# 29 unread products on TensorE behind the last y product, some on strips of 32 partitions

## The chip, the core and the metric

The kernel runs on one core of a Trainium2 chip. Its engines work side by side and are tied by semaphores: TensorE (PE) multiplies matrices, VectorE (DVE), ScalarE (ACT) and GpSimd (POOL) work on elements, and SyncE (SP) issues most of the DMAs. The metric is the device time of one execution in microseconds (us).

## The reference

The input `x` has 2048 tokens of 512 features. It is normalised (`xn`), and two branches work on that:

```
xn = layernorm(x)
h[t] = Lam_bar * h[t-1] + xn[t] @ B_bar.T          # 512 complex states, over all 2048 tokens
s  = 2 * real(h @ C.T) + xn * Dskip
g  = silu((gelu(xn @ w_gate) * (xn @ w_up)) @ w_down)   # 512 -> 1376 -> 512
out = x + s * g
```

All in bf16, one output of 2048 x 512.

## The kernel before, in words

**Tiling.** The tokens are cut into four slabs of 512 (`NS`), each of four tiles of 128 tokens (`M`). For a slab, `gate_tile` (products on line 535) makes the gate and up branches, `at_t` turns the result with a transposing DMA into `atT`, and `down_pair` (product on line 563, eleven products of 512 columns for a tile, the eleventh with 96 rows) multiplies it by `w_down` (`wd`) and applies silu on ScalarE (`g`, line 566). For the recurrence, `half` (products on line 614) projects to the states, VectorE rotates and scans them (lines 626 and 645) and leaves them in `hst`.

**The y step.** `y_part` joins the branches for a tile: ScalarE puts the skip term into a PSUM bank (line 574), TensorE adds eight products of `hst` and `C2` (line 578), VectorE multiplies by `g` (`yg`, line 584) and adds `x` (`ot`, line 585), and SP writes `ot` out (line 588). The very last tile of the last slab is cut into two halves of 256 columns (`y_tile`), so its 16 products are half as wide; they are TensorE's last ones.

**Order.** `Plan` records each step with what it reads and writes; `run` emits the steps in the hand-written list `ORDER`, one number a step, and each engine takes its instructions in that order. `SLOTS` says which buffer of a pool each group gets; pool `ps` is the six PSUM banks 0 to 5, and `bank()` takes the next entry of it. Line numbers of the profile are those of the kernel before. Line 914 is the end of the program: SP waits for the DMAs and engines, and then all engines meet at a barrier.

**Small products at the start.** `parameters` transposes two little tables of 4 and 8 rows (lines 671 and 672) between the full transposes of `head_t` (lines 386 and 399). The dummies on line 374 are seven products before any data is there.

Of the kernel before, what the change touches and what calls it, by code (L numbers as in the profile page):

```python
# [45 lines left out]
)  # L46
SLOTS = {
# [4 lines left out]
    ),  # L52
    "pp": (
        0, 1, 0, 1, 1, 1, 0, 0, 1, 0, 0, 1, 0, 1, 0, 1, 0, 1, 0, 1, 1, 0, 1, 0, 1, 1, 1, 0, 0, 0, 0, 1, 1, 0, 1, 0, 1, 0, 1,
# [94 lines left out]
def kernel(  # L149
# [18 lines left out]
    P = 128  # L168
# [8 lines left out]
    NS = S // TS  # L177
    M = TS // P
# [10 lines left out]
    V, A, G, T = nc.vector, nc.scalar, nc.gpsimd, nc.tensor  # L189
# [6 lines left out]
    def sb(name, shape, dt=BF16):  # L196
        return consts.tile(shape, dt, name=name)
# [5 lines left out]
    wd = sb("wd", [P, NFT, D])  # L203
# [6 lines left out]
    atT = sb("atT", [P, NFT, TS])  # L210
# [35 lines left out]
    def bank(part=False):  # L246
        pool = "pp" if part else "ps"
        g, i = pl.group(pool)
        return (pool, g), banks[SIZES["ps"] + i if part else i]
# [9 lines left out]
    def pe(n, cols, emit, reads=(), writes=(), **kw):  # L259
        return pl.add(PE, n * (cols + 6) / 2400.0, emit, reads, writes, lag=0.22, **kw)  # L260
# [108 lines left out]
    def dummies(k):  # L369
        held = [bank(True), bank(True), bank()]  # L370

        def f():
            for j in range(k):
                T.matmul(held[min(j, 2)][1][:], lhsT=warm[:, 0:P], rhs=warm, start=True, stop=True)
        pl.add(PE, k * 0.427, f, [], [b[0] for b in held], lag=0.22, not_before=0.6)

    def head_t(m):

        if m == 0:
            for i in range(2):  # L380
                key, ps = bank()
                tp = ps[:].bitcast(BF16)[:, 0 : D // 2].rearrange("p (k t) -> p k t", t=P)

                def f(i=i, tp=tp):
                    for k in range(2):
                        T.transpose(tp[:, k, :], xn[0][:, (2 * i + k) * P : (2 * i + k + 1) * P], ident[:])
                pe(2, P, f, [("xc", 0, i), "ident"], [key])
                dst = xcT[:, 2 * i : 2 * i + 2, 0:P]
                if i == 0:
                    dve(256, lambda tp=tp, dst=dst: V.tensor_copy(out=dst, in_=tp), [key], [("xcT", 0, 0)], rate=2.0)  # L390
                else:
                    acts(256, lambda tp=tp, dst=dst: act(out=dst, in_=tp, func=AF.Copy), [key], [("xcT", 0, 1)])
            return
        key, ps = bank(True)
        tp = ps[:].bitcast(BF16)[:, 0:D].rearrange("p (k t) -> p k t", t=P)

        def f():
            for k in range(KT):
                T.transpose(tp[:, k, :], xn[m][:, k * P : (k + 1) * P], ident[:])
        pe(KT, P, f, [("xc", m, 0), ("xc", m, 1), "ident"], [key])  # L400
        dve(512, lambda: V.tensor_copy(out=xcT[:, :, m * P : (m + 1) * P], in_=tp), [key], [("xcT", m, 0), ("xcT", m, 1)], rate=2.0, rank=310.0 - 20 * m)
# [143 lines left out]
    atTs = {}  # L545
# [22 lines left out]
    def y_part(s, m, c0, c1):  # L568

        w = c1 - c0  # L570
        key, bk = bank()
        ps = bk[:, 0:w]
        kk, skt = sks[s, m]
        acts(w, lambda: act(out=ps, in_=skt[:, c0:c1], func=AF.Copy), [kk], [key])  # L574

        def f():
            for j in range(2 * NPT):
                T.matmul(ps, lhsT=hst[s % 2][:, j // NPT, j % NPT, m * P : (m + 1) * P], rhs=C2[:, j // NPT, j % NPT, c0:c1],  # L578
                         start=False, stop=(j == 2 * NPT - 1), skip_group_check=True)
        pe(2 * NPT, w, f, [("hst", s % 2, 0), ("hst", s % 2, 1)] + C2S + [key], [key])  # L580
        gg, ig = g2s[s, m]
        gy, iy = pl.group("yg")
        go, io = pl.group("ot")
        dve(w, lambda: V.tensor_tensor(out=yg[iy][:, 0:w], in0=ps, in1=g2[ig][:, c0:c1], op=ALU.mult), [key, ("g2", gg)], [("yg", gy)])  # L584
        dve(w, lambda: V.tensor_tensor(out=ot[io][:, 0:w], in0=yg[iy][:, 0:w], in1=x_tok[:, s * M + m, c0:c1], op=ALU.add),  # L585
            [("yg", gy), ("x", s, m)], [("ot", go)], rate=2.0)
        mg = s * TS + m * P
        dma(SP, 0.35, 1.5, lambda: nc.sync.dma_start(out=out_td[mg : mg + P, c0:c1], in_=ot[io][:, 0:w]), [("ot", go)], [("out", s, m, c0)], svc=(2, 0.4, 0.9))

    def y_tile(s, m):  # L590
        cuts = (0, HD, D) if (s, m) == (NS - 1, M - 1) else (0, D)
        for c0, c1 in zip(cuts, cuts[1:]):
            y_part(s, m, c0, c1)
# [122 lines left out]


    dummies(7)
    center(0)
    head_t(0)  # L720
# [164 lines left out]
            down_pair(s, h)  # L885
    for m in range(M):
        y_tile(NS - 1, m)
    pl.run()


# [28 lines left out]
```

## Time and profile before

| | |
|---|---|
| three runs | 179.44, 179.39, 179.14 us (median 179.39) |
| profiled execution | 179.08 us, of which the span of its instructions 177.3 us |
| TensorE busy | 172.1 us (97% of the span), 834 products recorded |
| VectorE busy | 154.4 us (87%) |
| ScalarE busy | 133.0 us (75%) |
| granted TensorE clock, mean | 1.000 |

Times in the profile count from the span's first instruction. PE is the row of products and PEld that of weight loads, which overlap the products. A name like `PEldq` or `SPq` is the sequencer of that engine. A product's duration runs from its entering the array to its modelled end, and the next one enters before that, so that durations of neighbours overlap. A bracket such as `[0.20 <-issue]` gives the idle time before an instruction and what ended it; "issue" means that nothing the profile shows did.

### The profile page before, as it was taken

To read this page: it belongs to the slowest core of one execution; us is meant where nothing else is said; L and a number is where in the kernel's file an instruction comes from. 1 tells how busy PE (TensorE), PEld (TensorE's weight loads), DVE (VectorE), ACT (ScalarE), POOL (GpSimd) and SP (SyncE) were. 2 spreads that over 40 slices of the span, in tenths; PEclk is the share of its full clock that TensorE was granted. 3 is DMA by queue.
4 is the path that set the end of the run, shared out by engine and by line. 5 is a ranking of instruction groups with operands and counts; after the bars stand their busy time and mean duration, and the time that the engine had idled before them with its cause. 6 is when DMAs were issued, how large, how long until landed. Compare 5 with 4: busy or idle time off the path is not lost.

```text
span 177.3 us, 2419 instructions
## 1 busy us (share of the span) xinstructions
PE 172.1 (97%) x834; PEld 82.3 (46%) x849; DVE 154.4 (87%) x253; ACT 133.0 (75%) x246; POOL 10.7 (6%) x25
## 2 busy tenths in 40 slices
PE   8999999999999999999999999999999999999992
PEld 2544444454454444444444454444444444444451
DVE  3563799999999988999999699999999999999343
ACT  6779999989999999966698665735898860793310
POOL 2450510000200000001000000000000000000000
PEclk9999999999999999999999999999999999999999
DMA  5999998996092630040059050053007300550531
GB/s 151 290 361 211 170 300 192 305 225 135 0 190 54 129 71 4 0 81 0 0 115 127 25 111 0 0 125 71 0 12 154 86 0 4 133 119 0 113 118 30
DMA packets 47939, 18.66 MB, mean 105 GB/s; under 512 B 40280, under 2 KB 47288, under 8 KB 47928
## 3 DMA queue, kind: packets, MB, share of 16 engines
q1 hardware_dynamic: 47904, 18.52, 47.0%
q8 instruction: 6, 0.10, 0.2%
q14 instruction: 5, 0.04, 0.1%
q10 hardware_dynamic: 24, 0.00, 0.0%
HBM read 6.46 MB, written 2.10 MB: 48 GB/s over the span
## 4 chain that ended last, share of the span: by engine, by line
PE 91%; DMA 4%; SPq 1%; issue 1%; DVE 0%
PE bank L535 31%; PE bank L563 21%; PE bank L614 16%; PE bank L578 16%; PE bank L498 6%; DMA wu<-in_B_w_up_dram 3%; PE bank L461 2%; DMA x_tok<-in_A_x_dram 1%; SPq L287 1%; SPq L296 0%; DVE yg L584 0%; DVE ot L585 0%
## 5 line engine op out<-in xcount | busy, mean ns | idle before, releaser
L535 PEld LDWEIGHTS <-xnT 128*128 128x128 bf16 x288 | 28.1, 98 | 29.4
L563 PE MATMUL bank<-wd,atT 128*128 128x512 bf16 (+1 forms) x174 | 40.2, 379 | 0.1
L535 PE MATMUL bank<-wu,xnT 128*128 128x512 bf16 (+1 forms) x140 | 31.9, 356 | 0.1
L535 PE MATMUL bank<-wg,xnT 128*128 128x512 bf16 (+1 forms) x139 | 31.7, 356 | 0.3
L614 PE MATMUL bank<-xnT,BT 128*128 128x512 bf16 x128 | 30.9, 379 | 0.1
L645 DVE TENSOR_TENSOR_SCAN Fs<-rho,ini,W 128x512 bf16<-128x512 f32 x24 | 29.7, 1270 | 0.1
L578 PE MATMUL bank<-C,hst 128*128 128x512 bf16 (+1 forms) x134 | 29.7, 366 | 0.1
L563 PEld LDWEIGHTS <-atT 128*128 128x128 bf16 (+1 forms) x176 | 17.2, 98 | 20.3
L538 ACT ACTIVATE ubA<-bank 128x512 bf16<-128x512 f32 x24 | 14.6, 614 | 8.7 <-PE bank L535 8.3
L616 ACT ACTIVATE U<-bank 128x512 bf16<-128x512 f32 x32 | 19.0, 618 | 1.7 <-PE bank L614 1.7
L578 PEld LDWEIGHTS <-hst 128*128 128x128 bf16 x136 | 13.3, 98 | 14.0
L614 PEld LDWEIGHTS <-BT 128*128 128x128 bf16 x128 | 12.5, 98 | 14.3
L626 DVE TENSOR_TENSOR Q<-U,tab 128x4096 bf16<-128x4096 bf16 x8 | 18.3, 2286 | 0.7 <-ACT tab L714 0.6
L538 ACT ACTIVATE gtA<-bank 128x512 bf16<-128x512 f32 x24 | 14.8, 616 | 5.3 <-PE bank L535 4.6
L626 DVE TENSOR_TENSOR Q<-Fs,tab 128x4096 bf16<-128x4096 bf16 x8 | 18.3, 2285 | 0.1
L566 ACT ACTIVATE g<-bank 128x512 f32<-128x512 f32 x16 | 9.2, 594 | 12.2 <-PE bank L563 12.1
L584 DVE TENSOR_TENSOR yg<-bank,g 128x512 bf16<-128x512 f32 (+1 forms) x17 | 11.1, 654 | 5.1 <-PE bank L578 4.9
L538 ACT ACTIVATE ubB<-bank 128x352 bf16<-128x352 f32 x12 | 5.7, 475 | 6.5 <-PE bank L535 5.5
L837 ACT ACTIVATE junk<-x_tok 128x512 bf16<-128x512 bf16 x16 | 10.2, 648 | 0.0
L498 PE MATMUL bank<-wg,W 128*128 128x512 bf16 (+1 forms) x47 | 9.7, 356 | 0.1
L842 ACT ACTIVATE xna<-x_tok,nb,rs 128x512 bf16<-128x512 bf16 x12 | 9.5, 866 | 0.0
L574 ACT ACTIVATE bank<-sk 128x512 f32<-128x512 bf16 (+1 forms) x17 | 9.5, 576 | 0.1
(121 smaller groups left out, 189.7 us busy)
## 6 DMA issues: line engine op xcount, KB each, us to landing
out_dram<-ot SPq DMA_DIRECT2D x15, 128.0 KB, 1.7
x_tok<-in_A_x_dram SPq DMA_DIRECT2D x3, 512.0 KB, 9.3
wg<-in_B_w_gate_dram SPq DMA_DIRECT2D x1, 1376.0 KB
wd<-in_B_w_down_dram SPq DMA_DIRECT2D x1, 1280.0 KB, 6.6
wu<-in_B_w_up_dram SPq DMA_DIRECT2D x6, 128.0 KB, 3.2
x_tok<-in_A_x_dram SPq DMA_DIRECT2D x4, 128.0 KB, 2.3
wu<-in_B_w_up_dram SPq DMA_DIRECT2D x1, 352.0 KB, 3.5
wu<-in_B_w_up_dram SPq DMA_DIRECT2D x1, 256.0 KB, 5.2
```

The source lines that it names most:

```text
L498: T.matmul(ps[:, 0 : b - a], lhsT=xcT[:, k, m * P : (m + 1) * P], rhs=wt[:, k, a:b], start=(k == 0), stop=(k == KT - 1))
L535: T.matmul(ps[:, 0 : b - a], lhsT=xnT[:, s % 2, m, k, :], rhs=wt[:, k, a:b], start=(k == 0), stop=(k == KT - 1))
L538: acts(b - a, lambda: act(out=dst, in_=ps[:, 0 : b - a], func=AF.Copy if up else AF.Gelu_apprx_tanh), [key], [ok], table=None if up else " ...
L563: T.matmul(ps[:], lhsT=atT[:fs, k, iT * P : (iT + 1) * P], rhs=wd[:fs, k, :], start=(k == 0), stop=(k == NFT - 1))
L574: acts(w, lambda: act(out=ps, in_=skt[:, c0:c1], func=AF.Copy), [kk], [key])
L578: T.matmul(ps, lhsT=hst[s % 2][:, j // NPT, j % NPT, m * P : (m + 1) * P], rhs=C2[:, j // NPT, j % NPT, c0:c1], start=False, stop=(j == 2 ...
L584: dve(w, lambda: V.tensor_tensor(out=yg[iy][:, 0:w], in0=ps, in1=g2[ig][:, c0:c1], op=ALU.mult), [key, ("g2", gg)], [("yg", gy)])
L614: T.matmul(ps[:], lhsT=BT[:, ri, k, pt * P : (pt + 1) * P], rhs=xnT[:, s % 2, :, k, :], start=(k == 0), stop=(k == KT - 1))
L616: acts(512, lambda q=q, ri=ri, ps=ps: act(out=U[ui][:, ri, q, :], in_=ps[:], func=AF.Copy), [key], [("U", ug, q, ri)])
L626: dve(4096, lambda: V.tensor_tensor(out=Qf, in0=src.unsqueeze(1).to_broadcast(WQ), in1=table, op=ALU.mult), reads, ["Q"], rate=2.0)
L645: pl.add(DVE, 1.12 if s == 0 else 1.185, lambda ri=ri, q=q, pt=pt, first=first: V.tensor_tensor_scan(out=Fs[:, ri, q, :], data0=rho[:, pt ...
L837: acts(512, lambda i=i, fn=fn, sc=sc, m=m: act(out=junk()[:], in_=x_tok[:, s * M + m, :], func=fn, scale=sc, accum_out=sx[:, s, i, m : m + ...
```

## The change

A new step, `packed`, is the last in the plan and in `ORDER` (number 691). It takes four PSUM banks of pool `ps` (entries 1, 2, 4, 5) and multiplies pieces of the last tile's `atT` by pieces of `wd`. Each product begins and ends its own sum in its bank (`start` and `stop`); nobody reads these banks. All products are 512 columns wide:

- 3 of 128 rows into the first bank,
- four rounds of four products of 32 rows each, on partitions 0 to 31, 32 to 63, 64 to 95 and 96 to 127, each of the four into a bank of its own,
- 2 of 128 rows into the first bank,
- three times one of 96 rows (partitions 0 to 95, first bank) and one of 32 rows (partitions 96 to 127, fourth bank),
- 2 of 128 rows into the first bank.

That is 3 + 16 + 2 + 6 + 2 = 29 products, and each has its own weight load. In the built program a product of 32 rows carries a tile of 32 x 128 at its strip; those of 96 and 128 rows carry a tile of 128 x 128. The instruction streams of the other engines are unchanged, and that of TensorE is unchanged up to the last y product.

```diff
@@ ORDER and SLOTS
     683, 684, 690, 685,
+    691,
...
+        1, 2, 4, 5,
...
+    def packed():
+        held = [bank() for _ in range(4)]
+        gT, iT = atTs[NS - 1, M - 1]
+        wt, xt = wd, atT[:, :, iT * P : (iT + 1) * P]
+
+        def rows(b, r0, r1, k, cols=512):
+            pos = None if (r0, r1) == (0, P) else (r0, 0)
+            T.matmul(held[b][1][:, 0:cols], lhsT=xt[r0:r1, k, :], rhs=wt[r0:r1, k, 0:cols], start=True, stop=True, tile_position=pos)
+
+        def f():
+            for k in range(3):
+                rows(0, 0, P, k)
+            for k in range(4):
+                for b in range(4):
+                    rows(b, 32 * b, 32 * b + 32, k)
+            for k in range(2):
+                rows(0, 0, P, k)
+            for k in range(3):
+                rows(0, 0, 96, k)
+                rows(3, 96, P, k)
+            for k in range(2):
+                rows(0, 0, P, k)
+        pe(12, 512, f, ["wd0", ("atT", gT)], [h[0] for h in held])
...
     for m in range(M):
         y_tile(NS - 1, m)
+    packed()
     pl.run()
```

## The prediction

> **What bounds the kernel now.** I read the page first, then the chain that ended last in 165 to 178 us, the timeline of the last six microseconds, the closing instructions (line 914), and at last the rows that price a product, a weight load and a change of shape.
>
> The page's head, its slices and its chain:
>
> ```profile
> span 177.3 us, 2419 instructions
> ...
> PE   8999999999999999999999999999999999999992
> ...
> PE 91%; DMA 4%; SPq 1%; issue 1%; DVE 0%
> ```
>
> TensorE is busy in every slice up to the last one and is 91% of the chain. Only there, at the end, is it free: the last slice (4.4 us long) has a 2. The chain of waits in the last 13 us says what comes then:
>
> ```profile
> 164.97 4.96 PE bank L578 x23
> 169.94 2.38 PE bank L563 x11
> 172.31 1.76 PE bank L578 x16
> 174.08 0.02 issue
> 174.10 0.43 DVE yg L584
> 174.54 0.02 issue
> 174.56 0.29 DVE ot L585
> ```
>
> TensorE's last product ends at 172.31 + 1.76 = 174.07 us. VectorE then needs two steps and is done at 174.85; the output's DMA follows. Timeline of 171.8 to 177.3, and line 914 (the program's end) in three short windows with the waits of SP's queue:
>
> ```profile
> 172.15 1.91 PE L578 MATMUL bank<-C,hst 128*128 128x256 bf16 x16
> ...
> 174.08 1.14 SPq L588 DMA_DIRECT2D out_dram<-ot  x2
> ```
>
> ```profile
> L914 PEldq DRAIN  x1: 2373/2373/2373, 171.7 to 171.7; - x1
> ```
>
> ```profile
> L914 SPq EVENT_SEMAPHORE  x2: 28/28/28, 176.4 to 176.5; - x2
> ```
>
> ```profile
> SPq L914 <- DMA out_dram<-ot: 1.0, 2, 0.7
> ```
>
> The second of the two 64 KB DMAs is issued at 174.88, lands 1.5 us later (the page's landing time for that size), and SP's closing waits pass at 176.4. From there to the span's end, 177.3, is a barrier of all engines, 0.9 us. TensorE's sequencer stood in its DRAIN from 171.7 to 174.1, until its last product had ended, so the barrier needs TensorE too; it simply came 2.35 us before SP (176.42 - 174.07). **That 2.35 us is the cover for everything the change adds.**
>
> **The change, part by part.** The instruction streams of the other four engines are the same in both programs, and TensorE's is the same up to its last y product; behind it stand 29 products and 29 weight loads (the diff counts 3 + 16 + 2 + 6 + 2). Nothing is removed or moved. Nothing waits for their banks except the program's end.
>
> The waits it adds: the new products wait for the readers of four banks. The last of these is ScalarE's `g` (line 566), which runs from 172.35 to 172.95; the first product that needs that bank is the seventh of the new ones. The new stream can't begin before 174.07, so no wait is late, and nothing else is queued behind them. Cost 0; were that cover gone, the stream would shift by the delay.
>
> The price of one product with 512 columns: the first piece of the chain above gives 4.96 / 23 = 0.216 us. One with fewer rows costs the same, as the groups by form show (the first row has 128 rows, the second 96; 379 and 381 ns each):
>
> ```profile
> L563 PE MATMUL bank<-wd,atT 128*128 128x512 bf16 x158 | 36.9, 379 | 0.1
> ...
> L563 PE MATMUL bank<-wd,atT 96*128 96x512 bf16 x16 | 6.1, 381 | 0.1
> ```
>
> (379 ns is from entering to leaving; one follows the other at 0.216.) So rows left empty save nothing; only products that run beside each other would.
>
> *The 13 full products and those of 96 rows* (3 + 2 + 3 + 2, and the three 32-row partners of the 96-row ones): the built program gives a 96-row product the whole array as its tile, as a 128-row one, and its 32-row partner the fourth strip of it. Two that claim the same strip should not run together, so I count the three pairs as six: 13 x 0.216 = 2.80 us.
>
> *Four groups of four 32-row products.* No row of this trace shows two products beside each other. From one side a group can't take less than one product, 0.216; from the other, four in a row take 0.863. A floor nearer to the case is the weight loads, since each of the four has its own. The timeline around 10 us has four loads and products of 128 columns in a row:
>
> ```profile
> 10.27 0.39 PE L399 MATMUL bank<-ident,xna 128*128 128x128 bf16 x4
> 10.49 0.38 PE L461 MATMUL bank<-wu,W 128*128 128x512 bf16 x1
> ```
>
> From start to start (10.49 - 10.27) / 4 = 0.055 us for a load with its product. Four loads: 0.22 us, which is the value I take: 4 x 0.22 = 0.88 us. The Trainium skill ("TensorE: Matmul & The Clock Gate", Measured speedup vs the span model) gives 3.07 times for four row tiles of 32 rows and 512 columns; as an estimate that is 4 x 0.216 / 3.07 = 0.28 us for a group, and would put 0.25 us onto the sum.
>
> *Changes of tile shape.* In the new stream the tile goes from the whole array to strips ahead of the four groups and back behind them (2 changes), and changes at every step of the three pairs (6): 8 in all. Before has such a step in its first microseconds, where the 4-row transposes of line 671 follow full ones:
>
> ```profile
> 4.17 0.13 PEld L386 LDWEIGHTS <-xna 128*128 128x128 bf16 x2
> ...
> 4.50 0.10 PEld L671 LDWEIGHTS <-pv 4*128 4x128 bf16 x1 [0.20 <-issue]
> ```
>
> Loads otherwise start as soon as the product before has begun; here the load stood 0.20 us for nothing that the profile shows. The product before it began at 4.26, so start to start is 0.24; 0.10 of it is streaming (128 columns at the pace of those first microseconds, where 512 take 0.43). That leaves 0.14 us for the change, but at half the later pace, so 0.07 if all of it scales. I take the middle, 0.11: 8 x 0.11 = 0.88 us. Ends: 0 (the step was something else), and 0.26 (the pipe runs empty, 379 - 216 = 163 ns, and the load of 98 ns is not covered), 2.1 us in all.
>
> **Sum:** 2.80 + 0.88 + 0.88 = 4.56 us. TensorE ends at 174.07 + 4.56 = 178.63; with the closing 0.9 us the span is 179.53, 2.2 us more. In general the time grows by the added work less 2.33 us (177.3 - 0.9 - 174.07). The profiled execution took 179.08 us (177.3 of span and 1.8 around it), so it would take 181.3. The median of the three runs, 179.39, lies 0.3 above that execution, so I forecast **181.6 us** (+1.2%).
>
> **The rivals.**
> 1. *All strips work side by side and a change of shape is free.* For it: the step at 4.50 is a single one and at another pace. Against: its 0.20 us has no other releaser. With the pairs side by side too, 14 slots: 14 x 0.216 = 3.02, less 2.33: +0.7, 180.1 us; with the pairs one after another, 17 slots, 3.67: +1.3, 180.7 us.
> 2. *The strips do not run beside each other; the change doesn't do what its name says.* For it: no row shows two products at once, and products of 4 and 8 rows (lines 671, 672) are 47 ns apart though they hardly stream. Against: these two share a strip. 29 x 0.216 = 6.26: +3.9, 183.3 us; with the changes of shape 7.14: +4.8, 184.2 us.
> 3. *Not slower: it all fits under the landing of the last output.* TensorE has 2.35 us until SP's closing wait passes at 176.4. If the added stream takes no more than that, the span ends as before: 179.4 us. With 14 slots this asks for 0.168 us a slot or less. For it: the end is set by a DMA that the change doesn't touch. Against: 0.216 us over 23 products in a row, and 0.216 for 11 (2.38 / 11) right behind, so the fewest slots I can count need 3.02. The Trainium skill ("TensorE: Matmul & The Clock Gate", Back-to-back issue gap) speaks for it with some 131 ns for a product of 512 columns in a sustained stream of loads and products; by that 14 slots are an estimated 1.83 us and the change costs nothing. The trace's 0.216 disagrees.
>
> **How the numbers follow.** Forecast 0.48 (its own range, changes at 0.07 to 0.26 us and groups at 0.22 to 0.28, is 181.3 to 183.1); rival 1: 0.24; rival 2: 0.23; rival 3: 0.05. The range goes from just under rival 1, 180.0, to 183.4, which takes in rival 2 without the changes of shape; outside it are rival 3 and about half of rival 2, 0.17. A measurement of this kernel can tell about 0.2% (0.36 us) from no change; only rival 3 stays within that: same 0.05, slower 0.94, and 0.01 for faster, for which I see no mechanism.
>
> **What would show it.** In the profile after: the y products still end near 174.1, and DVE and the output's DMAs stand as before. SP's last closing wait would be ended by TensorE. In the packed groups, four products should start within about 0.2 us, and each of the eight changes should show as idle time before the weight load. If products of one group start 0.216 us apart, rival 2 holds; if the 32-row partner starts with its 96-row product, my count of 13 is wrong; if TensorE ends before 176.4, rival 3. Were the y products themselves late, or the clock lower, the sum would rest on a wrong start.

## The result and the profile after

| | before | after |
|---|---|---|
| runs | 179.44, 179.39, 179.14 us | 181.04, 181.06, 180.91 us |
| median | 179.39 us | 181.04 us |
| ratio, 95% interval | | 1.0094 [1.0071, 1.0117] |
| profiled execution, its span | 179.08, 177.3 us | 181.04, 179.3 us |

The change costs 1.65 us, 0.9%; 2.2 us were forecast (181.6, range 180.0 to 183.4). A later set of runs, told below, gave 1.0118 [1.0084, 1.0153], 2.1 us.

The chain that ended last in 165 to 180 us, of after (start, length, what; in the changed files the line numbers are shifted: 594 to 604 is the y product that stood on line 578, and 385 or 386 is the helper `rows`, on which all new products lie):

```profile
172.11 1.75 PE bank L604 x16
173.86 4.51 PE bank L386 x29
```

Before, this chain left TensorE behind the last y product and went on through VectorE. Now it stays on TensorE: 29 products in 4.51 us, from 173.86 to 178.37. The added products now decide when the program ends, as the waits of SP's queue in the last ten microseconds say:

```profile
SPq L941 <- PE bank L386: 2.7, 1, 2.7
...
SPq L941 <- DMA out_dram<-ot: 0.5, 1, 0.5
```

Before, SP's closing waits were for the output's DMA alone, 1.0 us, apart from the closing barrier, whose 0.6 us are the same in both; now the longest is for TensorE, and the DMA's has shrunk to 0.5. Line 941 is the program's end, as 914 was. From TensorE's end at 178.37 to the span's end at 179.3 there is the same 0.9 us as before.

The timeline of the new stretch, 173.5 to 179.3 us:

```profile
173.70 4.67 PE L386 MATMUL bank<-wd,atT 128*128 128x512 bf16 x29
173.87 1.14 SPq L614 DMA_DIRECT2D out_dram<-ot  x2
...
174.36 0.29 DVE L611 TENSOR_TENSOR ot<-yg,x_tok 128x256 bf16<-128x256 bf16 x1
174.44 0.55 PEld L386 LDWEIGHTS <-atT 32*128 32x128 bf16 x16 [0.42 <-issue]
175.41 0.33 PEld L386 LDWEIGHTS <-atT 128*128 128x128 bf16 x3 [0.42 <-issue]
...
176.48 0.10 PEld L386 LDWEIGHTS <-atT 96*128 96x128 bf16 x1 [0.23 <-issue]
176.80 0.09 PEld L386 LDWEIGHTS <-atT 32*128 32x128 bf16 x1 [0.23 <-issue]
177.12 0.10 PEld L386 LDWEIGHTS <-atT 96*128 96x128 bf16 x1 [0.23 <-issue]
...
```

Three things are to be seen. VectorE and the output's DMAs stand where they stood, as far behind the y products as before. The row of weight loads breaks at each change of tile shape, eight times in all (the lines of three breaks are left out here), and each time "issue" ended the idle time, that is, nothing the profile shows. And at the pairs the loads come 0.32 us apart (176.48, 176.80, 177.12), where products of one shape follow each other at 0.216: each change adds 0.10 us. The 32-row products among the groups by form of 173.9 to 179 us (behind the bar stand busy time and the mean ns of one):

```profile
L386 PE MATMUL bank<-wd,atT 32*128 32x512 bf16 x19 | 2.2, 378 | 0.0
```

One of them lasts as long as a product of 128 rows did before, 378 ns to 379, but 19 of them are done in 2.2 us. Three of the 19 stand alone in the pairs and take 3 x 0.38 = 1.1 us; the 16 of the groups so take 1.1 us together, as long as some four in a row.

### The profile page after: what moved, and what is told of

Read it like the earlier page. It is cut to its first block, busy times and chain, and to the rows that moved or that the text cites. A ratio compares the mean times of both kernels' runs of the same rounds, so it can differ in the third digit from the quotient of the medians.

```text
span 179.3 us, 2492 instructions
## 1 busy us (share of the span) xinstructions
PE 177.6 (99%) x878; PEld 83.9 (47%) x878; DVE 154.5 (86%) x253; ACT 132.8 (74%) x246; POOL 10.6 (6%) x25
## 4 chain that ended last, share of the span: by engine, by line
PE 99%; issue 0%
PE bank L561 31%; PE bank L589 21%; PE bank L604 15%; PE bank L640 15%; PE bank L524 7%; PE bank L487 4%; PE bank L386 3%; PE bank L376 2%; PE bank L425 1%; PE bank L412 0%; PE bank L697 0%; PE bank L698 0%
## 5 line engine op out<-in xcount | busy, mean ns | idle before, releaser
L561 PE MATMUL bank<-wu,xnT 128*128 128x512 bf16 (+1 forms) x144 | 32.5, 357 | 0.0
```

The source lines that it names most:

```text
L561: T.matmul(ps[:, 0 : b - a], lhsT=xnT[:, s % 2, m, k, :], rhs=wt[:, k, a:b], start=(k == 0), stop=(k == KT - 1))
```

## The experiments

The theory, as it stood after the first look: a slot takes 0.216 us, a group of four strips is one slot, a change of tile shape adds 0.10 us, and 2.33 us behind the last y product are free. The rivals deny one of these each. In every kernel only products that nobody reads are changed. Times are against runs of the kernel before on the same chip; a difference in us is the ratio less one, times the median of before (179.16 for the first four, 179.01 for the next three, 179.06 for the last four).

**1. The groups alone.**

```diff
-            for k in range(3):
-                rows(0, 0, P, k)
             for k in range(4):
                 for b in range(4):
                     rows(b, 32 * b, 32 * b + 32, k)
-            for k in range(2):
-                rows(0, 0, P, k)
...
```

> Only the four groups of four 32-row products stand behind the last y product; the other 13 products are left out. Theory (a group takes one slot of 0.216 us, a change of tile 0.10 us, and 2.33 us behind the last y product are free): 4 x 0.216 + 0.10 = 0.96 us, all of it covered, so no change from before (within 0.2%). Rival (strips take turns): 16 x 0.216 + 0.10 = 3.56 us, less 2.33: +1.2 us.

Measured: 1.0002 [0.9985, 1.0020]; no change. The last piece of its chain:

```profile
173.65 0.97 PE bank L386 x16
```

Sixteen products in 0.97 us, 0.87 without the change of shape: 0.22 us for four. The strips run side by side, and rival 2 of the prediction is out. The timeline of 173.57 to 173.60 us says what paces a group:

```profile
173.57 0.12 PEld L386 LDWEIGHTS <-atT 32*128 32x128 bf16 x8 [0.21 <-issue]
173.58 0.39 PE L386 MATMUL bank<-wd,atT 32*128 32x512 bf16 x4
```

Within 0.03 us eight loads and the four products of the first group began, and the eight loads took 0.12 us together. The loads of different strips run beside each other too; the next group comes 0.22 us later although its weights were there before. So a group is paced by the slot of its products, not by its four loads.

**2. Ten full products.**

```diff
-            for k in range(3):
+            for k in range(10):
                 rows(0, 0, P, k)
-            for k in range(4):
...
```

> Ten products of 128 rows in place of the 29. Theory (cover of 2.33 us until the last output has landed): 10 x 0.216 = 2.16 us, covered, so no change from before. Rival (the cover ends where VectorE ends, 0.8 us behind the last y product): 2.16 - 0.8 = +1.4 us. Second rival (products that nobody reads disturb the output's DMA): the landing of the last output takes longer than 1.5 us.

Measured: 0.9997 [0.9983, 1.0010]; no change. The chain of it, and SP's waits:

```profile
174.11 2.16 PE bank L386 x10
```

```profile
SPq L931 <- DMA out_dram<-ot: 1.0, 2, 0.7
```

TensorE works 2.16 us longer and is named as the last in the chain of instructions, yet SP waits 1.0 us for the output's DMA, the longest 0.7, as in before. The cover is that landing, not VectorE's end, and the added products did not make it longer.

**3. Pairs of 64 and 64 rows.**

```diff
             for k in range(3):
-                rows(0, 0, 96, k)
-                rows(3, 96, P, k)
+                rows(0, 0, 64, k)
+                rows(3, 64, P, k)
```

> The three pairs of 96 and 32 rows become pairs of 64 and 64 rows, both of one tile shape (64 x 128); all else as in the change. Theory (strips of one shape run beside each other, and only a change of shape costs): 14 slots x 0.216 + 4 changes x 0.10 = 3.42 us, less 2.33: +1.1 us on before, 0.5 less than the change. Rival (only the 32-row strips run beside each other, pairs take turns): 17 slots and 4 changes, 4.07: +1.7 us.

Measured: 1.0069 [1.0045, 1.0093], +1.2 us. In its trace the added stretch takes 3.45 us (3.42 expected by the theory, 4.07 by the rival):

```profile
173.98 3.45 PE bank L386 x29
```

The same number of products, 1.06 us less than in after (4.51): three slots fewer, since the two of a pair run beside each other, and four changes fewer. The pairs still alternate between the same two banks and between two places in the array, so neither of these is what a change costs; the shape is. The times alone would not settle it, since the interval reaches to +1.7; the trace does.

**4. The pairs sorted.**

```diff
             for k in range(3):
                 rows(0, 0, 96, k)
+            for k in range(3):
                 rows(3, 96, P, k)
```

> The same six products of the pairs in another order: first the three of 96 rows, then the three of 32 rows on one strip; all else as in the change. Theory (each change of tile shape costs 0.10 us; 4 changes are left of 8): 17 x 0.216 + 4 x 0.10 = 4.07 us, 0.4 less than the change, +1.2 to 1.3 us on before. Rival (a product with fewer rows than the array, in its own right, takes 0.32 us): as the change, +1.65 us.

Measured: 1.0102 [1.0080, 1.0124], +1.8 us: a miss, and on the face of it the rival's. The trace says otherwise, 4.09 us for the same 29 products, 0.42 less than after, and the loads now stand in runs:

```profile
174.04 4.09 PE bank L386 x29
```

```profile
175.59 0.76 PEld L386 LDWEIGHTS <-atT 128*128 128x128 bf16 x5 [0.42 <-issue]
176.78 0.33 PEld L386 LDWEIGHTS <-atT 32*128 32x128 bf16 x3 [0.42 <-issue]
```

What was wrong was the expectation's starting point: it took after's first 1.65 us as the point to count from, though the theory's own sum for after is 4.47 - 2.33 = 2.1, and for this kernel 4.07 - 2.33 = 1.7. Experiments 8 to 10 were made to settle that.

**5. One strip.**

```diff
-                    rows(b, 32 * b, 32 * b + 32, k)
+                    rows(b, 96, P, k)
```

> The four products of each group all use the strip of partitions 96 to 127 (same data, four banks as in the change). Theory (one strip takes one product at a time): 12 more slots x 0.216 = 2.6 us on the change, +4.2 us on before. Rival (what paces a group is its four weight loads, not the strip): as the change, +1.65 us.

Measured: 1.0376 [1.0332, 1.0419], +6.7 us; the median is 185.9. The rival (paced by the loads) is out, but the theory missed by 2.5 us. The 32-row products of 174 to 177.6 us, then the full ones from 178 us on, the granted clock by stretches (the last figure but two of each line, behind the five engines), and three loads of its pairs:

```profile
L386 PE MATMUL bank<-wd,atT 32*128 32x512 bf16 x15 | 3.4, 375 | 0.0
```

```profile
L386 PE MATMUL bank<-wd,atT 128*128 128x512 bf16 x4 | 2.1, 620 | 0.0
```

```profile
174.00:176.00 2.00, 1.95 (x10) 0.76 (x9) 0.55 (x2) 0.00 (x0) 0.00 (x0) 1.00 0.23 66
176.00:177.90 1.90, 1.90 (x10) 0.65 (x7) 0.00 (x0) 0.00 (x0) 0.00 (x0) 0.99 0.00 0
177.90:180.00 2.10, 2.10 (x6) 0.48 (x5) 0.00 (x0) 0.00 (x0) 0.00 (x0) 0.50 0.00 0
```

```profile
179.34 0.10 PEld L386 LDWEIGHTS <-atT 32*128 32x128 bf16 x1 [0.84 <-issue]
179.87 0.10 PEld L386 LDWEIGHTS <-atT 96*128 96x128 bf16 x1 [0.44 <-issue]
180.41 0.10 PEld L386 LDWEIGHTS <-atT 32*128 32x128 bf16 x1 [0.44 <-issue]
```

On one strip the products take turns at 0.216 us, as expected. But behind 3.5 us of them the granted clock is 0.50 and stays there to the end, and a full product takes 620 ns in place of 380. The added stretch by the theory is 4.47 + 12 x 0.216 = 7.06 us; the trace has 9.26, from 173.80, where the y products end, to 183.05 (one record at its start is missing):

```profile
173.80 0.22 PE bank L386
...
174.06 8.99 PE bank L386 x27
```

The 2.2 us between are the lost clock: the ten products behind the strips each take some 0.21 us longer. All four runs of this kernel lost it, with a mean granted clock of 0.980 to 0.989.

**6. Narrow pairs.**

```diff
-                rows(0, 0, 96, k)
-                rows(3, 96, P, k)
+                rows(0, 0, 96, k, 128)
+                rows(3, 96, P, k, 128)
```

> The six products of the pairs have 128 columns in place of 512; all else as in the change. Theory (a change of tile shape adds 0.10 us to the streaming, whatever its length): each of the six takes 0.16 in place of 0.316 us, 0.97 us less than the change, +0.65 us on before. Rival (the step takes some 0.31 us from start to start and hides the streaming): as the change, +1.65 us.

Measured: 1.0060 [1.0043, 1.0076], +1.1 us. The stretch is 3.55 us, from 173.79, where the y products end, to 174.06 + 3.28 (one record at its start is missing from the trace):

```profile
173.79 0.22 PE bank L386
...
174.06 3.28 PE bank L386 x27
```

That is 0.96 us less than after, as the theory has it (0.97): the change of shape adds its 0.10 us to a stream of 128 columns as to one of 512. The figure on before is again 0.4 above the expectation, which was counted from 1.65; from the theory's sum, 3.50 - 2.33, it is 1.2.

**7. Ahead of the last half of the last y tile.**

```diff
-    664, 669, 673, 647, 670, 687, 682, 665, 674, 688, 689, 675,
+    664, 669, 673, 647, 670, 687, 665, 674, 688, 689, 675, 691, 682,
```

> The same 29 products stand between the two halves of the last y tile, so that the last eight y products, VectorE and the output follow them. Theory (the 2.33 us are free only behind the last y product): the whole stream is on the path, 4.5 us, +4.5 us on before. Rival (the end of the program takes up such time wherever it arises): as the change, +1.65 us.

Measured: 1.0250 [1.0232, 1.0269], +4.5 us. Its chain from 172 us:

```profile
172.99 0.22 PE bank L385
...
173.26 4.24 PE bank L385 x27
177.50 0.89 PE bank L603 x8
...
178.41 0.44 DVE yg L609
```

The same products now stand ahead of work that the output waits for, and the whole stretch, 4.51 us from 172.99 to 177.50, is paid. The 2.33 us belong to the place, not to the products.

**8 to 10. The change once more, and the price of a change of shape by itself.**

Number 8 is the change as it stands. In 9, by turns, this stands between the first three and the last two full products, in place of the rest:

```diff
+            for k in range(10):
+                rows(0, 0, 96, k)
+                rows(3, 64, P, k)
```

And in 10, sorted:

```diff
+            for k in range(10):
+                rows(0, 0, 96, k)
+            for k in range(10):
+                rows(3, 64, P, k)
```

> The change as it stands, beside the next three kernels on one chip, since the pairs in sorted order came out at +1.8 us where +1.2 to 1.3 was expected, about where the change itself stood on another chip. Theory (the price of a tile change stands; the shift lies in where the y products end, which differs by some 0.2 us between executions): +1.5 to +2.1 us. Rival (the order of the pairs makes no difference): the same, so the next two tell these apart.

> In place of the groups and the pairs stand ten products of 96 rows and ten of 64 rows on the upper half of the array, by turns: 25 products and 20 changes of tile shape. Theory (0.216 us a product, 0.10 us a change): 5.4 + 2.0 = 7.4 us, less 2.33: +5.1 us on before. Rival (a change of shape costs nothing of its own in whole programs): 5.4 us, +3.1 us.

> The same 25 products, sorted: first the ten of 96 rows, then the ten of 64 rows, so that 2 changes of tile shape are left. Theory: 5.4 + 0.2 = 5.6 us, less 2.33: +3.3 us on before, 1.8 us under the kernel where they take turns. Rival (the order makes no difference): as that kernel.

Measured: the change 1.0118 [1.0084, 1.0153], +2.1 us; by turns 1.0290 [1.0247, 1.0334], +5.2 us; sorted 1.0197 [1.0154, 1.0240], +3.5 us. The added stretches, by turns first, then sorted, then the change:

```profile
174.00 7.49 PE bank L386 x25
```

```profile
174.06 5.61 PE bank L386 x25
```

```profile
173.73 4.51 PE bank L386 x29
```

25 products, once with 20 changes of shape and once with 2: (7.49 - 5.61) / 18 = 0.104 us a change, and the medians, 184.24 and 182.47, are 1.8 us apart. The order does matter. The change itself takes 4.51 us in both of its traces and stands at +2.1 here, which is the theory's sum; the first set's +1.65 was the low one of two, and the two intervals overlap.

**11. Half the array.**

```diff
-                    rows(b, 32 * b, 32 * b + 32, k)
+                    rows(b, 64, P, k)
```

> The 16 products of the groups have 64 rows on the upper half of the array, one behind the other, where the kernel with one strip of 32 had a quarter of the array at work and lost its clock. Theory (what holds the clock up is how much of the array works; half is enough): 12 more slots than the change, +4.2 us on before, clock 1.0 to the end. Rival (a half counts as idle too, or the small tile itself does it): the clock falls in the second half of the added stream, +5.5 to +7 us.

Measured: 1.0267 [1.0225, 1.0310], +4.8 us. The stretch and the clock:

```profile
174.31 7.09 PE bank L386 x29
```

```profile
174.50:178.00 3.50, 3.50 (x18) 1.41 (x16) 0.56 (x2) 0.00 (x0) 0.00 (x0) 1.00 0.13 37
```

Again 16 products in turn and eight changes of shape, 7.09 us against 7.06 by the sum, and the clock stays at 1.00, in all four runs. (The +4.2 of the expectation was again counted from 1.65; the sum gives 4.7.) So the loss in experiment 5 came with a quarter of the array at work, and the upper half was enough. Only the strip of partitions 96 to 127 was tried alone, so it is not shown that another quarter would lose the clock as well.

All of it in one table; the sum is slots x 0.216 + changes x 0.10:

| kernel | slots | changes | sum | stretch in the trace | sum less 2.33 | measured on before |
|---|---|---|---|---|---|---|
| groups alone | 4 | 1 | 0.96 | 0.97 | covered | 0.0 |
| ten full | 10 | 0 | 2.16 | 2.16 | covered | -0.1 |
| pairs of 64 | 14 | 4 | 3.42 | 3.45 | 1.1 | 1.2 |
| narrow pairs | 11 and 6 short | 8 | 3.50 | 3.55 | 1.2 | 1.1 |
| pairs sorted | 17 | 4 | 4.07 | 4.09 | 1.7 | 1.8 |
| the change | 17 | 8 | 4.47 | 4.51, 4.51 | 2.1 | 1.65, 2.1 |
| 25 sorted | 25 | 2 | 5.60 | 5.61 | 3.3 | 3.5 |
| half the array | 29 | 8 | 7.06 | 7.09 | 4.7 | 4.8 |
| 25 by turns | 25 | 20 | 7.40 | 7.49 | 5.1 | 5.2 |
| one strip | 29 | 8 | 7.06 | 9.26 (clock 0.50) | 4.7 | 6.7 |

No version beats the kernel before, and none could: what is added is read by nobody.

## Why the prediction was right, point by point

**The cover.** Forecast 2.35 us until SP's closing wait, 2.33 in the sum. Right: 2.16 us of added work cost nothing (experiment 2), 3.45 us cost 1.2 (experiment 3), and ahead of the output's last half nothing is covered (experiment 7).

**The added waits.** Forecast 0. Right: the first new product began 0.11 us behind the last y product, one slot of 256 columns, and the one that needed ScalarE's bank was not late.

**The 13 slots.** Forecast 2.80 us, with the pairs in turn. Right: in after the two of a pair are 0.32 us apart. Pairs of one shape do run side by side (experiment 3), so the reason given, that a 96-row product claims the whole array, fits; a 96-row product on a tile of just three strips was not tried.

**The groups.** Forecast 0.22 us each, from the pace of the weight loads. The size was right (0.87 us for four without the change of shape), the reason was not: in experiment 1 eight loads, two for each strip, take 0.12 us together, where eight at 0.055 would take 0.44, and each group waits for the slot of the one before, 0.216 us. That four loads at 0.055 come to nearly the same figure was luck. The factor of 3.07 of the Trainium skill ("TensorE: Matmul & The Clock Gate", Measured speedup vs the span model), which the prediction set beside it, would have made it 0.28; here the 16 products take the time of some four, a factor of 4.0 in a running stream (16 x 0.216 / 0.87).

**The changes of shape.** Forecast 0.11 us each, 0.88 in all; measured 0.104. The one row at the start gave 0.14 at half the later pace, and the doubt was whether it scales. In experiment 5, at clock 0.50, loads of the pairs are 0.54 us apart (179.34, 179.87, 180.41) and a plain slot is 0.43 (from 178.35 to 178.78), so a change is 0.11 there as well: it does not scale with the clock. The 0.14 was read somewhat too high, and the middle between it and 0.07 came near by luck. The Trainium skill ("TensorEngine Tiling (Array Packing)", Tiling Modes) says that a change of mode drains TensorE; the trace agrees in part: in after the load of a new shape starts 0.31 us behind the start of the product before it (176.17 to 176.48), so it is held back, but not until that product's modelled end, 0.38 us behind its start.

**The total.** Sum 4.56 forecast, 4.51 measured. The time came out 0.56 lower than forecast, 181.04 for 181.6, and the step that was off is the base: 0.05 lies in the sum; 0.21 in the start, since the y products ended at 173.86 in after's profiled execution and at 174.07 in before's, with the same instructions ahead of them (in the thirteen profiles they end between 173.65 and 174.31 in all but experiment 7, where they are moved); and 0.3 in the step from the profiled execution to the median, which was added as before had it, while after's profiled execution equals its median. The second set of runs, +2.1 us, stands at the forecast's +2.2.

**The rivals.** Rival 1 is out: changes have a price, and the 96-row pairs take turns. The time alone would not have told: its 180.7 us for pairs in turn lies nearer to the measured 181.04 than the forecast does. The stretch in the trace decides, 4.51 us where 17 slots without a price would take 3.67, and the 0.104 us of experiments 9 and 10. Rival 2 is out by experiment 1. Rival 3 held only for less added work: with 17 slots it would have needed 0.14 us a slot, and at the full clock products of 512 columns on the whole array follow each other at 0.216 in every trace. The 131 ns that the Trainium skill ("TensorE: Matmul & The Clock Gate", Back-to-back issue gap) gives for a product of 512 columns in a stream were seen between such products in no kernel.

## What to carry to other kernels

Behind the last instruction that the output needs there is a stretch, here the landing of the last DMA, in which an engine can work for nothing; read its length from what ends the closing waits, and count added work against that and not against the engine's busy share. Four products on four strips cost what one costs, but every change of tile shape costs 0.10 us, beside a stream of 128 columns as of 512, so products of one shape belong together. And where a difference is small, compare the stretch in the traces: in this case it came out at 4.51 us in both traces of the change, while the measured difference on before moved by 0.4 us between two sets of runs.

## What was not expected of the hardware

Sixteen 32-row products on one strip, 3.5 us of them with TensorE busy all the time, took the granted clock from 1.00 to 0.50; sixteen of 64 rows on half of the array, as long a stretch, left it at 1.00. (The groups of the change, on four strips at once, left it there too, but last only 0.9 us and so tell nothing of it.) Busy time in the profile therefore doesn't tell whether the clock will hold. The Trainium skill ("TensorE: Matmul & The Clock Gate", Part 1) has the clock follow how busy TensorE was in windows of some 3.4 us; that length fits the 3.5 us behind which the clock had fallen here, but that a quarter of the array at work did not hold the clock was learnt here. One kernel shows it, in all four of its runs; another strip was not tried, nor where between a quarter and a half the line lies.
